# Attention and two MLPs in one kernel: the conversion of the later weights is spread over other steps, and the output products take another order

## The chip, the core and the metric

The kernel runs on one core of a Trainium2 chip. The time is the device time of one execution in microseconds (us), as the median of several runs; a profiled execution gives the trace. The core's engines are TensorE (PE in the rows, its weight loads PEld), VectorE (DVE), ScalarE (ACT), GpSimd (POOL) and SyncE (SP), which issues all DMAs of this kernel. Each engine works through its instructions in the order in which the program wrote them.

## The reference

Three stages, all in float32, with weights that are stored as 64-bit floats:

```
k_p, v_p = mean of k, v over groups of 8 positions        # 576 -> 72 keys
attn = softmax(q k_p^T / 8) v_p                           # 8 batches x 8 heads x 576 positions x 64
x = attn as 4608 tokens x 512
x = (sigmoid(x w_gate) * (x w_val)) w_out                 # 512 -> 1536 -> 512
h = x w2_in                                               # 512 -> 2048
out = (h * cos(h)) w2_out                                 # 2048 -> 512
```

## The kernel before

**Tiling.** The 4608 tokens are worked in nine chunks of 512, numbered 0 to 8 (`c`). To keep float32 precision on TensorE each operand is split into a high and a low part of a shorter type, and each product is three matmuls: high by high, high by low, low by high. Making the parts is a cast on ScalarE (the high part) and a subtraction on VectorE (the low part, `split_lo`, L66). A 64-bit weight first goes through one more ScalarE instruction (`stage_exponent`, L143) and two bit operations on VectorE (`stage_bits`, L148 and L153).

**Gate stage (span 0 to 917).** For each chunk twelve gate steps run (`gv_step`), one for each block of 128 of the 1536 columns: 24 matmuls, a sigmoid on ScalarE, a product on VectorE. Gate and value sums have four PSUM banks together, two steps' worth. Beside the steps of chunk `c` the attention of chunk `c+1` is computed; what stands beside which step is written down by `plan`. At the end of a chunk the attention output goes through a last product (`px`), a cast and a subtraction into `xT`, from which the next chunk's gate products are made. Results go to DRAM (`gd`, `od`), those of chunks 1 to 8 in the sums that a Strassen-Winograd product needs (seven half-size products instead of eight), which GpSimd makes (`tg`).

**Far weights.** While chunks 1 to 7 run, the weights of the later stages are converted: the two output weights (`o2`, 16 blocks, and `o`, 12 blocks) and the cosine weight `i2` (16 blocks), two blocks at a time. For the output weights four Winograd sums of the pair are made on GpSimd and split as well. Everything is stored to DRAM (`wd`, `so`, `td`) and read back later. The generator `far_weights` is cut into half steps by `yield`; `far_step` first issues the stores that are ready and then runs one half step, once ahead of each gate step and once behind it, 24 times a chunk. A pair of `o2` or `o` takes eight half steps, a pair of `i2` six: 14 x 8 + 8 x 6 = 160 of the 168 there are. It works in four slots, `w24` to `w27` (each 4 KB a partition): raw blocks `a` in `w24` and `b` in `w25`, the four sums in `w26`, the split blocks one after the other in `w27`, and then the split sums in `w24` and `w25`, so that the next pair's loads into these wait for the stores of the sums.

**Chunk 8 of the gate stage** has no attention beside it. As its gate and value blocks are used for the last time, `refill` loads far weights into their slots: 12 blocks of `o`, then 16 of `i2`, the first four into `w24` to `w27` ahead of the chunk. Beside it the `o` products of chunk 0 run (`o_step`), from parts that the class `Ahead` fetches and splits.

**Cosine stage (917 to 1607).** For each chunk 16 steps (`h_step`): twelve matmuls (L838 to L840), a reduction of the angle, sine, square and a product. Beside chunks 0 to 6 the `o` products of the later chunks run in 84 units (`unit_go` fetches, casts to `up` and subtracts; `unit_step` multiplies). Beside chunks 7 and 8 the output products of chunk 0 run, one `y_step` behind every second step from step 3 of chunk 7 on (L1046 to L1048, parts `hp`), and three behind the last cosine step. At its last `y_step` four results `y` are copied out of PSUM into the four buffers `r` and stored.

**Output stage (from 1609).** `y_chunk` works chunks 1 to 8 with seven Winograd products each (L1026, L1031), in the order of `PRODUCTS`: accumulators A, B, A, C, A, B, A. `strip` prepares the operand `sp` two products ahead (a cast, L928, and a subtraction). Sums that are needed later are copied to `m` (`kept`, L959) in buffers `r` or `n`; results go to `y` in two buffers `sums`, which the cosine stage used for its own Winograd sums `s`.

Of the kernel before, what the change touches and what calls it, by code (L numbers as in the profile page):

```python
# [23 lines left out]
def attention_two_mlps(  # L24
# [22 lines left out]
    nc = tc.nc  # L47
# [16 lines left out]
    def split_lo(engine, lo, x, hi):  # L64
# [21 lines left out]
    sd = {c: dp.tile([7, P, PAIRS, HALF], F32, name=f"sd{c}") for c in range(1, NC)}  # L86
    wd = {
        (kind, j): dp.tile([P, 2, DM], F32, name=f"w{kind}_{j}")
        for kind, n in (("o2", NF2), ("o", NF), ("i2", NF2)) for j in range(n)
    }  # L90
    td = [dp.tile([P, 4, 2, HALF], F32, name=f"td{m}") for m in range(PAIRS)]

# [84 lines left out]

    def far_weights():

        def tile_(k, shape, dtype, name):  # L180
            return wp.tile(shape, dtype, tag=f"w{2 * NF + k}", name=name)

        def finished(k, kind, j, raw):
            t = tile_(k, [P, 2, DM], F32R, f"w{kind}_{j}")
            nc.scalar.copy(t[:, 0], words(raw, F32, 1))
            yield
            split_lo(nc.vector, t[:, 1], words(raw, F32, 1), t[:, 0])
            t = t.bitcast(F32)
            ready.append((wd[kind, j], t))
            if kind != "o":  # L190
                return
            if j < HF:
                ready.append((so[0][:, j], t[:, :, :HALF]))
            else:
                ready.append((so[5][:, j - HF], t[:, :, :HALF]))
                ready.append((so[6][:, j - HF], t[:, :, HALF:]))

        todo = [("o2", m, PAIRS) for m in range(PAIRS)] + [("o", m, HF) for m in range(HF)]
        todo += [("i2", m, PAIRS) for m in range(PAIRS)]
        for kind, m, step in todo:  # L200
            ja, jb = m, m + step
            a = load((wp, f"w{2 * NF}"), (kind, ja))
            yield
            b = load((wp, f"w{2 * NF + 1}"), (kind, jb))
            stage_exponent(a)
            yield
            stage_exponent(b)
            yield
            stage_bits([a, b])
            yield  # L210
            if kind == "i2":
                yield from finished(3, kind, ja, a)
                both = finished(2, kind, jb, b)
                next(both)
                yield
                next(both, None)
                continue
# [4 lines left out]
            sums = (  # L222
                ((ALU.subtract, a2, a1), (ALU.subtract, b2, t[:, 0]),
                 (ALU.subtract, b2, a2), (ALU.subtract, b1, t[:, 1])) if kind == "o2" else
                ((ALU.add, a2, b2), (ALU.subtract, t[:, 0], a1),
                 (ALU.subtract, a1, a2), (ALU.subtract, b1, t[:, 1]))
            )
            for k, (op, x, y) in enumerate(sums):
                nc.gpsimd.tensor_tensor(out=t[:, k], in0=x, in1=y, op=op)
            yield from finished(3, kind, ja, a)  # L230
            yield
            both = finished(3, kind, jb, b)
            next(both)
            for k in range(2):
                c = tile_(k, [P, 2, 2, HALF], F32R, f"t{kind}{m}_{k}")
                nc.scalar.copy(c[:, :, 0], t[:, 2 * k:2 * k + 2])
                yield
                if k == 0:
                    next(both, None)
                split_lo(nc.vector, c[:, :, 1], t[:, 2 * k:2 * k + 2], c[:, :, 0])  # L240
                c = c.bitcast(F32)
                if kind == "o2":
                    ready.append((td[m][:, 2 * k:2 * k + 2], c))
                else:
                    ready.extend((so[1 + 2 * k + i][:, m], c[:, i]) for i in range(2))

    def split(upto=None, n=2):

# [11 lines left out]
        stage_bits(some)  # L260
        done["bits"] += len(some)

    refills = [("o", f) for f in range(NF)] + [("i2", j) for j in PAIRED]

    def refill(tag):
        kind, j = refills.pop(0)
# [618 lines left out]
    def load_combined(m):  # L885
# [80 lines left out]
    def y_chunk(c, work):  # L966
# [13 lines left out]

        def after(n):

            if n in (0, 1, 2):
                which, name = (("A", "m1"), ("B", "m5"), ("A", "m6"))[n]
                for u in range(2):
                    keep[name, u] = kept(acc[which][u], f"{name}_{c}_{u}")
                if n == 0:
                    y[:] = [
                        hp_.tile([P, 2, C], F32, tag="sums", name=f"y{c}_{r}", bufs=2)
                        for r in range(2)  # L990
                    ]
                return
            if n < 6:
                which, name, rows, cols = {
                    3: ("C", "m1", 0, 0), 4: ("A", "m5", 1, 1), 5: ("B", "m6", 0, 1),
                }[n]
# [41 lines left out]
    def y_step(c, j, g):  # L1038
        w = block("o2", j)
        wh, wl = w[:, 0], w[:, 1]  # L1040
        if j == 0:
            po[c] = [bank("t", [P, DM], f"py{c}_{n}") for n in range(4)]
        for n in range(4):
            p = po[c][n]
            s = slice(n * P, (n + 1) * P)
            nc.tensor.matmul(p, g[:, 0, s], wh, start=j == 0, stop=False)  # L1046
            nc.tensor.matmul(p, g[:, 0, s], wl, start=False, stop=False)
            nc.tensor.matmul(p, g[:, 1, s], wh, start=False, stop=j == NF2 - 1)  # L1048
            if j == NF2 - 1:
                y = hp_.tile([P, DM], F32, tag="r", name=f"y{c}_{n}", bufs=4)  # L1050
                if n % 2:
                    nc.scalar.mul(y, p, -1.0)
                else:
                    nc.vector.tensor_scalar(
                        out=y, in0=p, scalar1=-1.0, scalar2=None, op0=ALU.mult
                    )
                nc.sync.dma_start(out[c * C + n * P:c * C + (n + 1) * P, :], y)

    with tc.manual_schedule():
# [89 lines left out]
        for c in range(NC):  # L1149
            last = c == NC - 1  # L1150
            beside = [[] for _ in range(NF)]
            if not last:
                steps, early = plans[c]
                for n in range(NF):
                    if c == 0:
                        beside[n] += early[n]
                    beside[n] += steps[n]
                    if c + 1 < NC - 1:
                        beside[n] += plans[c + 1][1][n]
            else:  # L1160
# [4 lines left out]
                for n in range(2 * NF, NSLOT):  # L1165
                    refill(f"w{n}")
                at.release()
                mp = tc.alloc_tile_pool(name="mp", bufs=1, side="left", reuse_waits="tile")
                pp[0] = tc.alloc_tile_pool(name="pp1", bufs=1, side="left", reuse_waits="tile")
            for at_f, f in enumerate(FOLDED if c else range(NF)):  # L1170
                tick()
# [5 lines left out]
                elif last:  # L1177
                    if at_f == NF - 1:
# [2 lines left out]
                            name="pp2", bufs=1, side="left", reuse_waits="tile"  # L1181
                        )
                    (unit_go if at_f == NF - 1 else go.go)()
                else:
                    split()
                    far_step()
                gv_step(c, f, 1 if c == 0 and f < FIRST else None)
                if last:
                    for kind in "gv":
                        refill(place[kind, f][1])  # L1190
                    for n in range((0, 0, 0, 1, 1, 1, 2, 2, 2, 2, 1, 0)[at_f]):
                        if n:
                            go.go()
# [30 lines left out]
        for c in range(NC):  # L1224
# [8 lines left out]
            for k, j in enumerate(PAIRED):  # L1233
# [2 lines left out]
                    unit_go()  # L1236
                else:
                    gy.go()
                if c and len(spare) < len(last_slots) and (c >= NC - 2 or k % 4 == 3):
                    load_last()  # L1240
                late.append(h_step(c, j))
                if len(late) > 1:
# [64 lines left out]
```

## Time and profile before

| | us |
|---|---|
| median of 3 runs (1940.66 to 1946.33) | 1942.33 |
| the profiled execution's own time | 1939.25 |
| its span, first to last instruction | 1937.4 |
| TensorE busy | 1794.7 (93%) |
| VectorE busy | 1128.1 (58%) |
| ScalarE busy | 908.8 (47%) |
| GpSimd busy | 548.7 (28%) |
| DMA: 414.28 MB, share of 16 engines | 66.0% |

The page gives busy time, so a stage in which an engine is 100% busy and one in which it waits are mixed in one share. The mean granted clock of TensorE is 0.962 of full speed (2.4 GHz); its other level is 1.2 GHz. The sixteen blocks of `i2` are stored and read back as `wi`, 32 transfers of 512 KB.

### The profile page before, as it was taken

The numbers are of one execution on the slowest core, as the hardware profiler recorded it, in microseconds if no ns is written. First come the engines' busy times: TensorE is split into PE (matmuls) and PEld (weight loads), VectorE is DVE, ScalarE is ACT, GpSimd is POOL, SyncE is SP. The second block draws the span as 40 slices with busy tenths as digits, with TensorE's granted clock in tenths as the row PEclk, the third lists the DMA queues.
The fourth block names the chain that finished last, engine by engine and source line by source line (L and its number), as shares of the span: only waits on it lengthen the run. The fifth ranks groups of instructions, "written<-read, shape, count | busy, mean of one in ns | idle before, by whom it ended". The sixth has DMA issues, their size and how long they took to land. (4 is left out here: it accounts for less than half of the span.)

```text
span 1937.4 us, 24756 instructions
## 1 busy us (share of the span) xinstructions
PE 1794.7 (93%) x8560; PEld 1496.4 (77%) x8560; DVE 1128.1 (58%) x1830; ACT 908.8 (47%) x1528; POOL 548.7 (28%) x656
## 2 busy tenths in 40 slices
PE   5888989888887999999889999999999998999999
PEld 4767867766775778888677888888887886888887
DVE  7675555555545575512456586686685654665565
ACT  6554435343434454411445556556554554444443
POOL 4104352625344332121001334334333441000000
PEclk8989989998988999999999999999999998999999
DMA  8435465647655665586776877877776678666664
GB/s 220 144 118 170 155 213 170 207 155 222 204 190 194 214 198 166 181 290 203 241 239 226 289 255 249 260 257 252 255 235 202 209 253 281 222 220 208 214 221 153
DMA packets 296350, 414.28 MB, mean 214 GB/s; under 512 B 55072, under 2 KB 231712, under 8 KB 296224
## 3 DMA queue, kind: packets, MB, share of 16 engines
q1 hardware_dynamic: 296224, 412.69, 66.0%
q8 instruction: 68, 1.11, 0.2%
q14 instruction: 58, 0.48, 0.1%
HBM read 250.61 MB, written 162.00 MB: 213 GB/s over the span
## 5 line engine op out<-in xcount | busy, mean ns | idle before, releaser
L553 DVE TENSOR_TENSOR g<-pv,g 128x512 f32<-128x512 f32 (+1 forms) x111 | 75.1, 676 | 336.8 <-ACT g L552 141.4
L844 DVE SCALAR_TENSOR_TENSOR r<-n,ph 128x512 f32<-128x512 int32 x144 | 98.9, 687 | 224.5 <-issue 98.1
L838 PE MATMUL ph<-x,wi 128*128 128x512 f32 x576 | 224.1, 389 | 0.0
L839 PE MATMUL ph<-x,wi 128*128 128x512 f32 x576 | 224.1, 389 | 0.0
L840 PE MATMUL ph<-x,wi 128*128 128x512 f32 x576 | 224.1, 389 | 0.0
L545 PE MATMUL pg<-xT,wg 128*128 128x512 f32 (+1 forms) x444 | 188.4, 424 | 35.2 <-ACT xT L529 30.8
L872 POOL TENSOR_TENSOR s<-r,r 128x256 f32<-128x256 f32 x64 | 76.1, 1188 | 453.6 <-DVE r L854 328.3
L850 ACT ACTIVATE r<-r 128x512 f32<-128x512 f32 x144 | 91.1, 633 | 237.2 <-DVE r L847 97.5
L66 DVE TENSOR_TENSOR sp<-sf,sp 128x1024 fp32r<-128x1024 f32 x112 | 133.0, 1229 | 94.8 <-ACT sp L928 94.8
L547 PE MATMUL pg<-xT,wg 128*128 128x512 f32 (+1 forms) x444 | 178.3, 402 | 1.2 <-DVE wg L66 1.2
L546 PE MATMUL pg<-xT,wg 128*128 128x512 f32 (+1 forms) x444 | 179.3, 404 | 0.0
L545 PE MATMUL pv<-xT,wv 128*128 128x512 f32 (+1 forms) x444 | 170.6, 384 | 0.0
L547 PE MATMUL pv<-xT,wv 128*128 128x512 f32 (+1 forms) x444 | 170.5, 384 | 0.0
L546 PE MATMUL pv<-xT,wv 128*128 128x512 f32 (+1 forms) x444 | 170.4, 384 | 0.0
L928 ACT CAST sp<-sf 128x1024 fp32r<-128x1024 f32 x112 | 112.3, 1055 | 75.3 <-PE py_A L1031 28.6
L545 PEld LDWEIGHTS pg<-xT,wg 128*128 128x128 f32 x444 | 89.3, 201 | 54.2 <-ACT xT L529 31.9
L1026 PE MATMUL py_A<-tc,sp 128*128 128x512 f32 x384 | 122.5, 401 | 5.9 <-ACT sp L928 5.9
L838 PEld LDWEIGHTS ph<-x,wi 128*128 128x128 f32 x576 | 108.2, 188 | 22.5
L840 PEld LDWEIGHTS ph<-x,wi 128*128 128x128 f32 x576 | 108.1, 188 | 22.5
L839 PEld LDWEIGHTS ph<-x,wi 128*128 128x128 f32 x576 | 108.1, 188 | 22.4
L552 ACT ACTIVATE g<-pg 128x512 f32<-128x512 f32 (+1 forms) x111 | 64.9, 585 | 116.6 <-PE pg L547 61.2
L847 DVE SCALAR_TENSOR_TENSOR r<-n,r 128x512 f32<-128x512 int32 x144 | 107.8, 749 | 5.0
(180 smaller groups left out, 4160.8 us busy)
## 6 DMA issues: line engine op xcount, KB each, us to landing
sf<-sd SPq DMA_DIRECT2D x112, 512.0 KB
so<-so SPq DMA_DIRECT2D x84, 512.0 KB
uf<-od SPq DMA_DIRECT2D x168, 256.0 KB
sd<-s SPq DMA_DIRECT2D x64, 512.0 KB
wo<-wo SPq DMA_DIRECT2D x56, 512.0 KB
od<-tg SPq DMA_DIRECT2D x48, 512.0 KB
wi<-wi SPq DMA_DIRECT2D x32, 512.0 KB
sd<-r SPq DMA_DIRECT2D x64, 256.0 KB
```

The source lines that it names most:

```text
L66: engine.tensor_tensor(out=lo, in0=x, in1=hi.bitcast(F32), op=ALU.subtract)
L545: nc.tensor.matmul(p, wh, x[:, 0, kb], start=kb == 0, stop=False)
L546: nc.tensor.matmul(p, wh, x[:, 1, kb], start=False, stop=False)
L547: nc.tensor.matmul(p, wl, x[:, 0, kb], start=False, stop=kb == KB - 1)
L838: nc.tensor.matmul(p, wh, x[kb][:, 0], start=kb == 0, stop=False)
L839: nc.tensor.matmul(p, wh, x[kb][:, 1], start=False, stop=False)
L840: nc.tensor.matmul(p, wl, x[kb][:, 0], start=False, stop=kb == KB - 1)
L844: nc.vector.scalar_tensor_tensor(out=r, in0=n, scalar=-C1, in1=p, op0=ALU.mult, op1=ALU.add)
L847: nc.vector.scalar_tensor_tensor(out=r, in0=n, scalar=-C2, in1=r, op0=ALU.mult, op1=ALU.add)
L850: nc.scalar.activation(r, r, AF.Sin, scale=0.5)
L928: nc.scalar.copy(t[:, 0, h * w:(h + 1) * w], got[c, n, h])
L1026: nc.tensor.matmul(p, x[:, 0, m, s], w, start=fresh and m == 0, stop=False, skip_group_check=True,)
```

## The change

The far conversion takes only the two output weights and gives each pair twelve half steps. Both raw blocks load in the first; nothing is done in the second. The four sums are written by GpSimd into the words of the raw blocks that the bit operations have used up (every second word). Split blocks and split sums take turns in `w26` and `w27`, with an empty half step behind the blocks and two behind the sums:

```diff
-        todo += [("i2", m, PAIRS) for m in range(PAIRS)]
         for kind, m, step in todo:
             ja, jb = m, m + step
-            a = load((wp, f"w{2 * NF}"), (kind, ja))
+            a, b = (load((wp, f"w{2 * NF + i}"), (kind, j)) for i, j in enumerate((ja, jb)))
             yield
-            b = load((wp, f"w{2 * NF + 1}"), (kind, jb))
+            yield
             stage_exponent(a)
-            yield
             stage_exponent(b)
             yield
             stage_bits([a, b])
             yield
...
-            t = tile_(2, [P, 4, HALF], F32, f"t{kind}{m}")
+            t = [words(x, F32, 0)[:, h * HALF:(h + 1) * HALF] for x in (a, b) for h in range(2)]
...
             for k, (op, x, y) in enumerate(sums):
-                nc.gpsimd.tensor_tensor(out=t[:, k], in0=x, in1=y, op=op)
-            yield from finished(3, kind, ja, a)
+                nc.gpsimd.tensor_tensor(out=t[k], in0=x, in1=y, op=op)
+            first = plain(2, kind, ja, a)
             yield
-            both = finished(3, kind, jb, b)
...
+            plain_low(kind, ja, first)
+            second = plain(3, kind, jb, b)
+            yield
+            plain_low(kind, jb, second)
+            yield
+            yield
+            first = summed(2, 0, kind, m, a)
+            yield
+            summed_low(0, kind, m, first)
+            second = summed(3, 1, kind, m, b)
+            yield
+            summed_low(1, kind, m, second)
+            yield
+            yield
```

`plain` and `summed` make the cast into slot 2 (`w26`) or 3 (`w27`), `plain_low` and `summed_low` the subtraction, and queue the stores.

The cosine weights are no longer stored and read back. `i2_weights` loads them in chunk 8 into four places of a buffer that the first stage's output tiles use later (`x2`), converts them and writes them straight to the slots where `h_step` reads them: `w24` to `w27`, then the slots that the last six gate steps give free (`refill` hands these over once the twelve `o` blocks are placed). It is called twice a gate step, and once a cosine step of chunk 0:

```diff
+        for n, j in enumerate(PAIRED):
+            at = n if n < 4 else 11 + 5 * (n - 4) // 4
+            for later, fn, args in (
+                (4, low, (n, j)), (0, begin, (n, j)), (2, convert, (n,)), (3, high, (n, j)),
+            ):
+                events.setdefault(at + later, []).append((fn, args))
+        order_ = {low: 0, high: 1, convert: 2, begin: 3}
+        for n in range(max(events) + 1):
+            for fn, args in sorted(events.get(n, ()), key=lambda e: order_[e[0]]):
+                fn(*args)
+            yield
...
                     (unit_go if at_f == NF - 1 else go.go)()
+                    next(i2)
...
                     for kind in "gv":
                         refill(place[kind, f][1])
+                    next(i2)
...
+                if c == 0:
+                    next(i2, None)
+                elif len(spare) < len(last_slots) and (c >= NC - 2 or k % 4 == 3):
                     load_last()
```

`begin` is the load, `convert` the exponent and the two bit operations, `high` the cast and `low` the subtraction. The first four blocks begin at calls 0 to 3, the other twelve at calls 11 to 24.

In the output stage the second and the fourth product change places, C before B; chunk 0's `y` goes into the two buffers `sums`, two results in each; and its first output product stands behind step 5 of cosine chunk 7, so that four stand behind the last cosine step:

```diff
-        ("A", 0, "b11"), ("B", 1, 0), ("A", 2, 1), ("C", 5, "b21"),
+        ("A", 0, "b11"), ("C", 5, "b21"), ("A", 2, 1), ("B", 1, 0),
...
-                y = hp_.tile([P, DM], F32, tag="r", name=f"y{c}_{n}", bufs=4)
+                if n % 2 == 0:
+                    pair = hp_.tile([P, 2, DM], F32, tag="sums", name=f"y{c}_{n}", bufs=2)
+                y = pair[:, n % 2]
...
-                elif k % 2 and (k > 1 if not last else k < 13):
+                elif k % 2 and (k > 3 if not last else k < 13):
```

## Rows read from the trace of the kernel before

**Rows 1.** Busy us (instructions) of each engine by stretch, TensorE's clock, DMA

```profile
146.00:647.00 501.00, 433.31 (x2023) 357.79 (x2022) 268.69 (x536) 208.55 (x368) 219.02 (x263) 0.91 0.60 190
647.00:739.00 92.00, 86.25 (x414) 70.35 (x414) 57.69 (x112) 43.35 (x76) 33.25 (x42) 0.96 0.59 184
739.00:819.00 80.00, 80.00 (x397) 67.39 (x395) 44.75 (x92) 36.25 (x61) 18.85 (x24) 1.00 0.56 181
819.00:917.00 98.00, 98.00 (x434) 81.16 (x433) 18.98 (x28) 16.51 (x29) 18.42 (x24) 1.00 0.77 252
```

**Rows 2.** TensorE's waits, us, times, longest: 146 to 739, then chunk 6 alone

```profile
PE pg L545 <- ACT xT L529: 30.8, 5, 7.8
PE psc L419 <- ACT qT L408: 16.2, 3, 7.3
...
PE pg L545 <- ACT xT L529: 3.1, 1, 3.1
```

**Rows 3.** ScalarE's waits for DMAs over the whole span, us, times, longest

```profile
ACT raw_o L143 <- DMA raw_o<-in_moe_w_out_dram: 108.1, 24, 9.3
ACT raw_i L143 <- DMA raw_i<-in_moe_w_in_dram: 42.2, 13, 6.0
ACT wo L185 <- DMA so<-wo: 29.8, 6, 8.1
```

**Rows 4.** Timeline in chunk 5: start, us, instruction, [idle before <- released by]

```profile
556.89 0.84 SPq L176 DMA_DIRECT2D so<-to  x2
561.89 0.33 SPq L128 DMA_DIRECT2D raw_o<-in_moe_w_out_dram  x1
565.54 0.67 ACT L143 ACTIVATE raw_o<-raw_o 128x512 f32<-128x512 f32 x1 [3.77 <-DMA raw_o<-in_moe_w_out_dram]
...
598.61 1.81 PE L419 MATMUL psc<-kbd,qT 128*128 128x144 f32 x6 [7.33 <-ACT qT L408]
```

**Rows 5.** Instructions on the raw `o` blocks: ns min/median/max, first and last start

```profile
L143 ACT ACTIVATE raw_o<-raw_o x28: 652/667/690, 155.1 to 602.9; 128x512 f32<-128x512 f32 x28
L153 DVE SCALAR_TENSOR_TENSOR raw_o<-raw_o x28: 679/685/1225, 164.6 to 605.9; 128x512 int32<-128x512 int32 x28
L229 POOL TENSOR_TENSOR to<-raw_o x14: 852/1180/1318, 165.3 to 608.4; 128x256 f32<-128x256 f32 x14
```

**Rows 6.** Busy times as in rows 1, at the start of chunk 8

```profile
822.00:835.00 13.00, 13.00 (x59) 10.78 (x58) 3.40 (x6) 3.06 (x5) 2.88 (x4) 1.00 0.90 288
```

**Rows 7.** TensorE's timeline at the start of the cosine stage

```profile
936.34 0.79 PE L794 MATMUL po_A<-up,so 128*128 128x512 f32 x1 [3.39 <-ACT up L754]
...
948.95 0.50 PE L795 MATMUL po_B<-up,so 128*128 128x512 f32 x1 [0.93 <-DVE up L66]
```

**Rows 8.** Timelines of VectorE and TensorE at the first output products

```profile
1487.54 1.89 DVE L66 TENSOR_TENSOR hp<-h,hp 128x512 fp32r<-128x512 f32 x3
1488.27 0.80 PE L1048 MATMUL py<-wo,hp 128*128 128x512 f32 x1 [4.12 <-DVE hp L66]
...
1491.42 0.39 PE L1046 MATMUL py<-wo,hp 128*128 128x512 f32 x1
1491.65 0.40 PE L1047 MATMUL py<-wo,hp 128*128 128x512 f32 x1
```

**Rows 9.** Busy times as in rows 1, behind two waits of TensorE

```profile
1488.00:1491.50 3.50, 3.23 (x8) 2.59 (x9) 3.31 (x6) 1.52 (x4) 0.07 (x1) 0.52 0.97 339
1629.00:1634.80 5.80, 5.62 (x16) 4.32 (x17) 4.72 (x4) 3.90 (x6) 0.00 (x0) 0.50 0.50 138
```

**Rows 10.** The chain that ended last (first row), timelines of TensorE and ScalarE at the handover

```profile
1615.32 4.80 DMA sd<-s
...
1622.31 0.73 PE L1026 MATMUL py_B<-tc,sp 128*128 128x512 f32 x2 [2.64 <-DMA tc<-td]
...
1626.92 1.23 ACT L959 COPY m<-py_A 128x512 f32<-128x512 f32 x2 [7.34 <-DMA out_dram<-y]
...
1629.14 1.22 PE L1026 MATMUL py_A<-tc,sp 128*128 128x512 f32 x2 [5.87 <-ACT sp L928]
...
1634.81 0.63 PE L1026 MATMUL py_A<-tc,sp 128*128 128x512 f32 x2
```

More of the change, by code (lines that the diff above doesn't have):

```diff
@@ L88, in attention_two_mlps @@
         (kind, j): dp.tile([P, 2, DM], F32, name=f"w{kind}_{j}")
-        for kind, n in (("o2", NF2), ("o", NF), ("i2", NF2)) for j in range(n)
+        for kind, n in (("o2", NF2), ("o", NF)) for j in range(n)
     }
@@ L178, in far_weights, with place_, high @@
     def far_weights():
-        def tile_(k, shape, dtype, name):
+        def place_(k, shape, dtype, name):
             return wp.tile(shape, dtype, tag=f"w{2 * NF + k}", name=name)
-        def finished(k, kind, j, raw):
-            t = tile_(k, [P, 2, DM], F32R, f"w{kind}_{j}")
-            nc.scalar.copy(t[:, 0], words(raw, F32, 1))
-            yield
-            split_lo(nc.vector, t[:, 1], words(raw, F32, 1), t[:, 0])
-            t = t.bitcast(F32)
+        def high(k, shape, name, x, hi):
+            t = place_(k, shape, F32R, name)
+            hi = hi(t)
+            nc.scalar.copy(hi, x)
+            return t, x, hi
@@ L189, in finished, with low, plain, plain_low @@
+        def low(t, x, hi, lo):
+            split_lo(nc.vector, lo(t), x, hi)
+            return t.bitcast(F32)
+        def plain(k, kind, j, raw):
+            return high(k, [P, 2, DM], f"w{kind}_{j}", words(raw, F32, 1), lambda t: t[:, 0])
+        def plain_low(kind, j, made):
+            t = low(*made, lambda t: t[:, 1])
             ready.append((wd[kind, j], t))
-            if kind != "o":
-                return
-            if j < HF:
+            if kind == "o" and j < HF:
                 ready.append((so[0][:, j], t[:, :, :HALF]))
-            else:
+            elif kind == "o":
@@ L195, in finished, with summed, summed_low @@
                 ready.append((so[5][:, j - HF], t[:, :, :HALF]))
                 ready.append((so[6][:, j - HF], t[:, :, HALF:]))
+        def summed(k, n, kind, m, raw):
+            return high(
+                k, [P, 2, 2, HALF], f"t{kind}{m}_{n}",
+                words(raw, F32, 0).rearrange("p (o n) -> p o n", o=2), lambda t: t[:, :, 0],
+            )
+        def summed_low(n, kind, m, made):
+            t = low(*made, lambda t: t[:, :, 1])
+            if kind == "o2":
+                ready.append((td[m][:, 2 * n:2 * n + 2], t))
+            else:
+                ready.extend((so[1 + 2 * n + i][:, m], t[:, i]) for i in range(2))
@@ new lines, in far_weights, with i2_weights, begin, convert @@
+            second = plain(3, kind, jb, b)
[11 more added lines that the diff above has]
+            yield
+    free_i2 = []
+    def i2_weights(hold):
+        made = {}
+        def begin(n, j):
+            raw = hold[:, n % 4]
+            nc.sync.dma_start(
+                raw.rearrange("p (kb c) -> p kb c", kb=KB),
+                w2_in[:, j * P:(j + 1) * P].rearrange("(kb p) c -> p kb c", p=P),
+            )
+        def convert(n):
+            stage_exponent(hold[:, n % 4])
+            stage_bits([hold[:, n % 4]])
+        def high(n, j):
+            tag = free_i2.pop(0)
+            t = wp.tile([P, 2, DM], F32R, tag=tag, name=f"wi2{j}")
+            nc.scalar.copy(t[:, 0], words(hold[:, n % 4], F32, 1))
+            made[j] = t
+            place["i2", j] = wp, tag
+        def low(n, j):
+            t = made.pop(j)
+            split_lo(nc.vector, t[:, 1], words(hold[:, n % 4], F32, 1), t[:, 0])
+            blocks["i2", j] = t
+        events = {}
+        for n, j in enumerate(PAIRED):
[9 more added lines that the diff above has]
+            yield
@@ L261, in split @@
         done["bits"] += len(some)
-    refills = [("o", f) for f in range(NF)] + [("i2", j) for j in PAIRED]
+    refills = [("o", f) for f in range(NF)]
     def refill(tag):
+        if not refills:
+            free_i2.append(tag)
+            return
         kind, j = refills.pop(0)
@@ L981, in after @@
         def after(n):
[L983 to L984 removed]
+            if n in (0, 2, 3):
+                which, name = {0: ("A", "m1"), 2: ("A", "m6"), 3: ("B", "m5")}[n]
                 for u in range(2):
@@ L1164, in attention_two_mlps @@
                 far_stores()
-                for n in range(2 * NF, NSLOT):
-                    refill(f"w{n}")
+                free_i2.extend(f"w{n}" for n in range(2 * NF, NSLOT))
                 at.release()
                 mp = tc.alloc_tile_pool(name="mp", bufs=1, side="left", reuse_waits="tile")
+                i2 = i2_weights(
+                    mp.tile([P, 4, 512], I64, tag="x2", name="raw_i2", bufs=2)
+                )
                 pp[0] = tc.alloc_tile_pool(name="pp1", bufs=1, side="left", reuse_waits="tile")
```

32 lines of the change are left out of this document (5 added, 27 removed).

## The prediction

> **What bounds the kernel now.** I read the page first, then the busy times by stretch, then what TensorE waited for, then the timelines of the stretches that have waits. TensorE is the engine that decides: in chunk 7 (739 to 819) it is busy 80.00 of 80.00 us, in chunk 8 98.00 of 98.00, at a granted clock of 1.00 [rows 1]. Where it isn't full, something is to be had. Chunks 1 to 5 (146 to 647) take 501 us with 433.31 busy, so 67.7 idle, and the clock there is 0.91; chunk 6 takes 92 us with 5.75 idle and a clock of 0.96 [rows 1]. All six do nearly the same products. What differs is the far conversion beside them: the pairs of the two output weights in chunks 1 to 5, the cosine weights alone in chunk 6. From 146 to 739 the largest waits of TensorE are for ScalarE: 30.8 us for `xT` and 16.2 for `qT`; in chunk 6 alone 3.1 for `xT` [rows 2].
>
> ScalarE has little work there (208.55 busy of 501), but it works in program order, and it stands still for DMAs of the far conversion: 108.1 us for raw loads of the output weight, 29.8 for stores out of w27, which has to be empty before the next block is written into it [rows 3]. One pair shows the chain: the stores of the converted sums leave at 556.89, the load into the slot that one of them empties only at 561.89 (SyncE stood still between), ScalarE's exponent instruction waits for it until 565.54. In the next pair ScalarE again waits for a load, `qT` comes behind it, and TensorE idles 7.33 us, until 598.61 [rows 4].
>
> **Part 1, the far pairs.** Instructions per pair stay: 2 exponents, 4 casts, 4 bit operations, 4 subtractions, 4 GpSimd sums. Three waits go. The next loads go into w24 and w25, which now hold the sums in place and are last read by a subtraction two half steps earlier, so no load stands behind a store. Both loads start a whole gate step before the first exponent (some 8 us; 92 us by 12 steps [rows 1]); the one that left at 561.89 had landed by 565.54, 3.7 us [rows 4]. Each cast into w26 or w27 comes two half steps after the store that empties it, again a gate step. At the end of a chunk the last half step only stores, so that nothing of the far work stands on ScalarE ahead of the `xT` casts. The sums are written with a gap of one word; the trace has no such GpSimd write. I cost it between 0 and as much as the sum itself again, 1.2 us each (L229, up to 1.18 [rows 5]); with four sums a pair and two gate steps before the cast that reads them, I take 0.
>
> Fourteen pairs by 12 half steps are 168, just the 7 chunks by 24, so chunks 1 to 7 all carry two pairs each, where before 1 to 5 carried three and 6 four cosine pairs. That is less than chunk 6 carried on ScalarE and VectorE, and chunk 6 still waited on raw cosine loads (42.2 us in all over 13 waits [rows 3]). Chunk 6 is therefore my model: 92 us at most. Its floor is chunk 6 without its loss of clock: 4% of 92 us is 3.7, so 88.3 with all its waits (80, as in chunk 7, is out of reach, since that has no keys and values and one tile less [rows 1]). I take 91.5 for five of them and 89.5 for chunk 3, which has one tile less: 547 against 593, that is -46. If nothing but chunk 6's own rate comes, 6 by 92.5 (the page's stretches are cut to whole us), it is -38; if the floor comes, -593 + 6 x 88.3 = -63. Chunk 7 carries heavier pairs than before beside a TensorE without idle time: +0.5 (0 to +2).
>
> **Part 2, the cosine weights.** Sixteen stores and sixteen reloads of 512 KB go, 16.8 MB of 414; DMA isn't the limit of the gate chunks (share 0.60 [rows 1]), so this is worth nothing there by itself. In chunk 8 and the first cosine steps ScalarE gets 16 exponents and 16 casts (0.667 for both, 21 us), and VectorE 32 bit operations and 16 subtractions (0.685 for all, 33 us) [rows 5]. Twelve or thirteen sixteenths fall into chunk 8, where VectorE is busy 18.98 and ScalarE 16.51 of 98 us [rows 1]: hidden, as long as no instruction blocks. The block that can is the exponent, which waits for a raw load and stands ahead of the sigmoid. At the chunk's start four raw loads (2.1 MB) come on top of what goes there now, while the four reloads ahead of the chunk go and later ones move. The stretch 822 to 835 moved 288 GB/s at a DMA share of 0.90 [rows 6], 3.7 MB; 5.8 would take 20 us, so that the fourth load lands some 7 us late and a sigmoid about 4 us. One gate step here is 24 matmuls at 0.23 [rows 8], 5.5 us, and the gate and value products of two steps fit into their four banks, so that TensorE has a gate step of slack: +1 (0 to +6).
>
> The Trainium skill (DMA: Bandwidth & Descriptors, Specifications) puts what a core can move to and from HBM at about 358 GB/s; a short stretch with 339 at a share of 0.97 [rows 9] comes near that, the 288 at 0.90 don't. By its figure the same 5.8 MB would take 16 us, the last load would be 3 us late and the term 0, so the sum 1 us less; I go by the rows.
>
> In the first five cosine steps the rest comes on two engines on which TensorE already waits: 3.39 us for the cast `up`, then 0.93 for its subtraction in every second unit [rows 7]. A step gets 1.3 us more of ScalarE and 1.9 of VectorE, four times. Nothing hidden would be 4 x 1.9 = +8, all hidden 0: I take +4. On the other side SyncE is no longer held by reloads that wait for the last gate products, which could pull the 3.39 in; I leave it as the lower bound, -3.
>
> **Part 3, the output products start two steps later.** In chunk 7 of the cosine stage TensorE waits 4.12 us for the first `hp`, and the next seven matmuls, from 1488.27 to 1491.42, stand 0.45 apart where those behind stand 0.23; the granted clock is 0.52 in that stretch, nearly all of it the lower level (1.2 GHz) [rows 9]. 1.5 us more, together 5.6. The three `hp` subtractions start at 1487.54 [rows 8]. Two cosine steps of 2.7 us (twelve matmuls at 0.23) put ahead bring TensorE there at about 1489, when two of the three are done. -5 (-3 to -6). The product left out comes in the tail, the same work.
>
> **Part 4, the handover to the output products.** TensorE waits 2.64 us for the last `tc` load and 5.87 for `sp`, and the 5.67 us from 1629.14 to 1634.81 carry four blocks of which one takes 0.7 at full clock (two matmuls of 512 and two of 256 columns, 0.23 and 0.12), at a clock of 0.50 [rows 9]: 2.9 more, 11.4 us in all. The cast `sp` stands behind `m`, which is written to a buffer that `y` has left to its store, and waits for that store until 1626.92 [rows 10]. Now `y` takes the two `sums` buffers, and `m1` finds its own free. The second pair of `y` has to wait for the last `sd<-s` store, which left at 1615.32 and landed 4.8 us later; with four products in the tail this comes one product, 2.7 us, earlier against TensorE: 1617.5 in the old clock. Then come the copy of `y`, two of `m` and one cast: some 1620.5, and TensorE ends the second product at 1620.2. C as second product needs no `tc`, so that the 2.64 go. Late next is the subtraction behind that cast, 1.2 us. 11.4 less about 2.4 is -9 (-11 to 0, when the wait only changes its buffer). In the steady part the order of products changes nothing that TensorE waits for: 0.
>
> **Sum.** -46 + 0.5 + 1 + 4 - 5 - 9 = -54.5. The profiled execution took 1939.25 us with a span of 1937.4, which gives 1885; its time is 3 us under the median of the runs, so 1888.
>
> **Rivals.** First, the wait at the chunk's end stays. The 30.8 us for `xT` are the largest share of TensorE's waits [rows 2], and the chain of product, cast, subtraction and next product is there without any far work; chunk 6 shows it at 3.1, with cosine casts on ScalarE. If it stays at 7, four to five boundaries keep 4 us and the low clock after it (1.5 as in rows 8), some 25 us: gate chunks at -21 and 1913. Against it: ScalarE's own rows put a far cast directly ahead of `xT`.
>
> Second, the handover's wait only moves: `y` now waits for the `sums` store, and the first output tile for the four `y` stores, which took until 1626.9. Without Part 4's gain the time is 1897. For it speaks that two DMAs stand in a row there, against it that the first is three steps old.
>
> Third, the slower end: the cosine weights stall ScalarE. All 16 exponents in chunk 8 wait for loads in a stretch that starts at 288 GB/s [rows 6], and each holds back a sigmoid or a cosine cast. The longest wait on a raw cosine load was 6.0 us, the mean 3.2 [rows 3]. With one gate step of slack already spent, 16 by 4 us is 64 in place of the 5 above, and the time 1947; it decides from 3.7 us a block on (54.5 and 5, by 16). Against it: after the fourth block no load is begun for seven half steps, and ScalarE has 80 us to spare.
>
> A fourth, that the new pauses change nothing because another wait of the gate chunks was as late (keys on GpSimd, scores on VectorE), would leave only the tail's -14, and the upper bounds of the cosine weights (6 + 8 + 2) take these back: 1944. Chunk 6 speaks against it.
>
> **How the numbers follow.** Forecast 0.60, with 1873 to 1905 as its own bounds; first rival 0.19; second 0.10; third 0.07; fourth 0.04. Under 0.3% (6 us) this kernel can't be told from unchanged. The first three are faster (0.89), the third rival slower (0.07), the fourth within 0.3% (0.04). The range reaches from near the floor of the gate chunks (1871; with the lower bound of the cosine start 1864), 1868, to the first rival with the upper bounds of the cosine start, 1922.
>
> **What would show it.** Right: no wait of ScalarE for `so<-wo` or `wo<-wo`, raw waits under 30 us in all, chunks 1 to 6 near 91 us with TensorE at a clock of 0.96 or more; no wait of 4 us at the first `hp`; `m` without a wait for `out_dram<-y`. Wrong: `xT` waits of 7 us still there; idle time of TensorE in chunk 8; over 10 us of it in the first five cosine steps.

## The result and the profile after

The changed kernel takes 1829.3 us (median of 4 runs, 1827.95 to 1830.81) against 1941.51 for the kernel before on the same chip (median of 4): 0.942 of before, 95% interval 0.940 to 0.944. The change is about twice the 54.5 us that were forecast, and it lies below the range. The span fell by 109.2 us, from 1937.4 to 1828.2. Split at the start of the last sigmoid of each gate chunk, then of the first cast `n` of a cosine chunk and of the first product of the output stage (us):

| stretch | before | after | difference | forecast |
|---|---|---|---|---|
| to the end of chunk 0 | 145.8 | 147.8 | +1.9 | 0 |
| gate chunks 1 to 6 | 593.5 | 490.3 | -103.2 | -46 |
| chunk 7 | 79.4 | 79.4 | 0 | +0.5 |
| chunk 8 | 97.9 | 97.9 | 0 | +1 |
| cosine chunk 0 | 125.7 | 127.3 | +1.5 | +4 |
| cosine chunks 1 to 6 | 434.8 | 434.9 | 0 | 0 |
| cosine chunks 7 and 8 with the last of chunk 0's products | 131.8 | 133.1 | +1.4 | -5 |
| output stage | 328.3 | 317.5 | -10.8 | -9 |

Chunk 0 does the same as before; over the profiles of the changed kernel and its variants below its end lies between 146.0 and 148.8, so its +1.9 is taken as scatter. What is left is one large term, the gate chunks, and the handover. The busy times of the same stretches as in [rows 1], of the changed kernel (us of the stretch, then busy us and instructions of TensorE, its weight loads, VectorE, ScalarE, GpSimd, then the granted clock, DMA share, GB/s):

```profile
148.00:556.00 408.00, 405.36 (x2025) 339.67 (x2024) 251.37 (x499) 196.17 (x340) 199.44 (x248) 1.00 0.60 189
556.00:638.00 82.00, 82.00 (x413) 67.84 (x412) 50.14 (x102) 40.95 (x72) 36.72 (x47) 1.00 0.62 200
638.00:717.00 79.00, 79.00 (x391) 66.57 (x391) 47.35 (x91) 36.48 (x60) 26.18 (x34) 1.00 0.52 178
717.00:815.00 98.00, 98.00 (x434) 81.17 (x433) 41.21 (x63) 30.40 (x52) 20.63 (x24) 1.00 0.80 268
```

Chunks 1 to 5 hold the same products as before (2025 records for 2023) in 408 us in place of 501, and TensorE is busy 405.36 of them at a clock of 1.00, where it had 433.31 of 501 at 0.91. Busy time itself went down by 28 us: before, part of it was matmuls at the lower clock. Chunk 8 has VectorE at 41 us for 19 and ScalarE at 30 for 17 [rows 1], and TensorE is as full as it was. What TensorE waited for from 148 to 717, all of it, against [rows 2]:

```profile
PE px L584 <- DVE aT L66: 2.6, 1, 2.6
```

ScalarE's waits for DMAs there, against [rows 3] (us, times, longest):

```profile
ACT raw_o L143 <- DMA raw_o<-in_moe_w_out_dram: 16.0, 13, 3.7
ACT to L186 <- DMA wo<-wo: 12.2, 6, 3.1
ACT to L186 <- DMA so<-wo: 3.4, 3, 2.1
```

They didn't vanish, but they make only 31.6 us (with 4.5 more for `raw_i`, from chunk 8 on), each is short, and none reaches TensorE. Before, the far conversion's waits were longer than [rows 3] shows, since its rows leave out the other stores from `w27`:

```profile
ACT wo L185 <- DMA wo<-wo: 29.4, 6, 8.5
```

With them it was 209.5 us over the whole span, 20.2 of the 42.2 for `raw_i` in chunk 6 and 14.9 in chunk 7.

### The profile page after: what moved, and what is told of

Same layout as the page of the kernel before. It is cut to its first block, busy times and chain, and to the rows that moved or that the text cites. A ratio compares the mean times of both kernels' runs of the same rounds, so it can differ in the third digit from the quotient of the medians.

```text
span 1828.2 us, 24685 instructions
## 1 busy us (share of the span) xinstructions
PE 1764.3 (97%) x8560; PEld 1477.5 (81%) x8560; DVE 1135.8 (62%) x1830; ACT 913.0 (50%) x1528; POOL 542.5 (30%) x656
## 5 line engine op out<-in xcount | busy, mean ns | idle before, releaser
L66 DVE TENSOR_TENSOR sp<-sf,sp 128x1024 fp32r<-128x1024 f32 x112 | 132.9, 1229 | 80.8 <-ACT sp L984 80.7
L601 PE MATMUL pg<-xT,wg 128*128 128x512 f32 (+1 forms) x444 | 179.8, 405 | 2.0 <-ACT e L519 2.0
L603 PE MATMUL pg<-xT,wg 128*128 128x512 f32 (+1 forms) x444 | 172.7, 389 | 1.1 <-DVE wg L66 1.1
L602 PE MATMUL pg<-xT,wg 128*128 128x512 f32 (+1 forms) x444 | 172.3, 388 | 0.0
L66 DVE TENSOR_TENSOR up<-uf,up 128x1024 fp32r<-128x1024 f32 x84 | 102.4, 1219 | 6.2 <-ACT up L810 6.2
```

The lines of the kernel that those rows point to most:

```text
L66: engine.tensor_tensor(out=lo, in0=x, in1=hi.bitcast(F32), op=ALU.subtract)
L601: nc.tensor.matmul(p, wh, x[:, 0, kb], start=kb == 0, stop=False)
L602: nc.tensor.matmul(p, wh, x[:, 1, kb], start=False, stop=False)
L603: nc.tensor.matmul(p, wl, x[:, 0, kb], start=False, stop=kb == KB - 1)
```

## Experiments

All are the changed kernel with one edit, unless said. Times are medians of two to five runs; the kernel before ran beside each on the same chip, at 1943 to 1947.

**e1: the old pair code, cosine weights still in chunk 8**

`far_weights` is that of the kernel before, without the cosine weights. Against that kernel:

```diff
-        todo += [("i2", m, PAIRS) for m in range(PAIRS)]
...
-            if kind == "i2":
...
-                continue
```

> The changed kernel, but with the pair code of before for the two output weights (eight half steps, old slots); the cosine weights stay in chunk 8. Theory A: each old pair stops ScalarE on its own loads and stores, and that costs TensorE idle time and then its clock. Then chunks 1 to 4 stay at 97 to 101 us as before, chunk 5 at some 95 (its last third is free), chunks 6 and 7, now without any far work, come to 80 to 82 and 79; the time is some 1915 us. Rival B: the cosine conversion with its stores and reloads was what loaded the gate stage; then chunks 1 to 5 fall to 90 or less and the time is under 1880. Chunk 6 also tells whether its 92.5 us of before were its own products and waits (it stays above 88) or the cosine conversion (80 to 83).

1928.04 us, 0.991 of before (95% interval 0.987 to 0.994). The chunks 1 to 7 take 101.4, 97.9, 103.5, 101.0, 100.1, 82.8 and 79.4 us.

```profile
147.00:651.00 504.00, 436.24 (x2023) 360.14 (x2022) 266.06 (x531) 206.65 (x363) 217.35 (x264) 0.91 0.59 187
651.00:734.00 83.00, 83.00 (x418) 68.69 (x417) 38.63 (x89) 34.40 (x60) 28.73 (x41) 1.00 0.34 102
```

Theory A holds, though the time is 13 us over its 1915: chunk 3 is slower than it said, and chunk 5, whose last third is free, takes 100.1 for some 95. Moving the cosine weights gives chunks 1 to 5 nothing. It gives chunk 6 everything: without far work it takes 83 us and TensorE doesn't idle, so its 92 us [rows 1] were no floor but the cosine conversion of before. That is the number on which the forecast stood.

**e2 and e5: the old slots, spaced**

The old pair code with empty half steps; the edit is shown against that code (e1):

```diff
             b = load((wp, f"w{2 * NF + 1}"), (kind, jb))
-            stage_exponent(a)
             yield
+            yield
+            stage_exponent(a)
             stage_exponent(b)
...
             yield from finished(3, kind, ja, a)
             yield
+            yield
...
+            yield        # e2: three, e5: two
+            yield
```

> As the changed kernel with the old slots (sums in w26, split blocks both in w27, split sums in w24 and w25), but with twelve half steps: one more behind the loads, one behind the first store, three at the end. Theory A1: spacing alone is enough, since every cast and load then comes a gate step or more behind the DMA that it needs; chunks 1 to 6 at 80 to 84 us, time 1828 to 1842. Rival A2: the slots matter, since loads still go where stores have to leave first; chunks at 86 to 92, time 1865 or more.

1854.25 us: chunks 1 to 6 at 80.8 to 83.9, but chunk 8 at 113.0. The edit had made thirteen half steps a pair.

> The kernel of e2 with two empty half steps at the end of a pair in place of three. That one took thirteen half steps a pair (182 of the 168 there are), so that the last pair was converted at once at the start of chunk 8, which took 113 us for 98. Theory: with twelve, chunk 8 comes back to 98 and chunks 1 to 6 stay at 80 to 84 us, time 1832 to 1842; spacing alone then brings nearly all of the gate stage's gain. Rival: what chunks 1 to 6 gained in e2 came from the thirteenth half step, and they rise to 86 or more, time over 1855.

1828.68 us: chunks 1 to 6 at 490.2 us together, chunk 8 at 97.9. Spacing alone does all that the change does to the gate stage; the new slots and the sums in place aren't needed for it.

**e3: the new slots without the empty half steps**

```diff
             yield
-            yield
             stage_exponent(a)
...
             plain_low(kind, jb, second)
             yield
-            yield
...
             summed_low(1, kind, m, second)
-            yield
-            yield
```

> The changed kernel without its four empty half steps, so eight half steps a pair in the new slots, chunks 1 to 5 carrying three pairs. Theory A1 (spacing decides): the exponent stands half a gate step, about 3.5 us, behind a load that takes 5 to 8 us to land, and the casts one half step behind the stores; chunks 1 to 4 at 93 to 101 us, time 1890 to 1915. Rival A2 (the slots decide): loads no longer stand behind stores, so that chunks 1 to 4 come to 82 to 88, time 1835 to 1860.

1874.44 us; chunks 1 to 5 at 87.6, 93.5, 86.9, 90.8 and 93.2. Neither number was met: with pairs as dense as before, the new pair code (slots, sums in place, both loads first) is worth half. What TensorE waited for in chunks 1 to 5:

```profile
PE pg L597 <- ACT xT L581: 19.1, 4, 6.5
PE px L580 <- ACT qT L460: 5.6, 2, 4.3
PE psc L471 <- ACT qT L460: 3.4, 3, 1.6
PE px L580 <- DVE aT L66: 3.4, 2, 2.1
PE px L580 <- ACT aT L560: 0.9, 1, 0.9
```

e3 and e1 also tell waits from work. In chunks 1 to 5 both run the same number of instructions (VectorE 531, ScalarE 364 and 363), e3 as follows:

```profile
147.00:599.00 452.00, 419.57 (x2023) 348.22 (x2022) 260.85 (x531) 209.48 (x364) 210.52 (x263) 0.96 0.65 208
```

ScalarE's waits for the far conversion's DMAs there, e1 and then e3:

```profile
ACT raw_o L143 <- DMA raw_o<-in_moe_w_out_dram: 95.9, 22, 9.5
ACT wo L185 <- DMA so<-wo: 31.6, 6, 8.1
ACT wo L185 <- DMA wo<-wo: 29.4, 6, 8.6
...
ACT raw_o L143 <- DMA raw_o<-in_moe_w_out_dram: 47.2, 19, 6.0
ACT to L186 <- DMA so<-wo: 31.9, 7, 7.7
ACT to L186 <- DMA wo<-wo: 21.2, 8, 6.0
```

They fall from 156.9 us to 100.3, and TensorE's idle time from 67.8 to 32.4, with as much work beside it.

**e6 and e7: one empty half step moved to the end of the pair**

```diff
             yield
-            yield                    # e6: behind the loads
             stage_exponent(a)
...
             plain_low(kind, jb, second)
             yield
-            yield                    # e7: behind the first stores
...
+            yield                    # both: at the end
```

> The changed kernel with the empty half step behind the loads moved to the end of the pair, so that the two exponents come one half step, 3 to 4 us, behind loads that land in 5.0 to 8.5 us (median 6.4). ScalarE's waits for raw loads rise from 16 us to 60 to 100. Theory A: such a wait stands ahead of a sigmoid and costs TensorE what goes over its gate step of slack, little in itself; chunks 1 to 6 rise by 0 to 4 us each, time 1830 to 1853. Rival: pauses don't matter behind loads (the gain is the stores'), time within 2 us of the changed kernel, 1829.

> The changed kernel with the empty half step behind the first stores moved to the end of the pair, so that the cast of the sums into w26 comes one half step, 3 to 4 us, behind the issue of the store that empties it. ScalarE's waits for wo<-wo and so<-wo rise from 14 us to 40 to 70. Theory A: chunks 1 to 6 rise by 1 to 4 us each, time 1833 to 1853, more than e6, since the wait can hold a cast of the attention too. Rival: within 2 us of 1829.

1824.20 and 1829.86 us; chunks 1 to 6 at 487.4 and 488.0. Both theories A fall: ScalarE waits longer for stores in e7 (33.6 us from 148 to 632 in place of 13.4), and TensorE doesn't notice. In e6 the raw waits rose only to 24.1 us, not to 60. Its time is below the rival's too (1827 to 1831), but 3.9 of the 6.6 us by which its span is shorter lie in chunk 0 and cosine chunk 0, which the edit doesn't touch.

**e11 and e12: all empty half steps at the end**

```diff
-            yield                    # e12 only: the four of the change
...
+            for _ in range(4):       # at the end of the pair;
+                yield                # e11: code of e1, e12: new slots
```

> The old pair code and the old slots, its eight half steps as dense as before, then four empty ones; cosine weights in chunk 8. Theory D (the number of pairs in a chunk decides): two pairs a chunk stop ScalarE as long each as before (some 12 us), but TensorE has time to catch up in the empty steps and none of it falls on the xT casts at the chunk's end; chunks 1 to 6 at 82 to 88 us, time 1830 to 1865. Theory S (the distance inside a pair decides): a wait of 4 to 9 us costs TensorE the same wherever it stands, two thirds of the 100 us of loss remain; chunks at 92 to 96, time 1890 to 1910.

> The new slots with all four empty half steps at the end of the pair, the eight others as dense as in e3. Theory D: chunks 1 to 6 at 80 to 83 us, time within 5 us of the changed kernel, 1824 to 1834. Theory S: the waits of e3 stay (100 us of ScalarE's in 14 pairs), chunks at 84 to 87, time 1850 to 1862.

1835.36 and 1825.41 us. Theory D holds: what counts is how far apart the pairs are, hardly where the pause stands inside one. In e11 the code of a pair is that of before, word for word, and TensorE idles 3.7 us in chunks 1 to 5 instead of 67.7.

```profile
148.00:558.00 410.00, 406.29 (x2028) 339.78 (x2027) 250.94 (x499) 195.41 (x340) 200.22 (x246) 1.00 0.59 188
```

ScalarE's waits for DMAs in the same stretch of e11:

```profile
ACT raw_o L143 <- DMA raw_o<-in_moe_w_out_dram: 21.9, 9, 5.6
ACT wo L185 <- DMA wo<-wo: 21.6, 5, 6.7
ACT wo L185 <- DMA so<-wo: 7.3, 2, 5.0
```

Single waits of 5 to 6.7 us are still there, and pass. What changed is that the raw waits fell from 108.1 us for 14 pairs [rows 3] to 21.9 for some ten. By the code a pair's loads no longer stand right behind the last stores of the pair ahead.

**e13: ten half steps**

```diff
-            for _ in range(4):       # of e12
+            for _ in range(2):
                 yield
```

> New slots, eight half steps and two empty ones at the end, so 140 of 168 half steps and a pair that no longer ends with a chunk. Theory T (a threshold: what stays inside TensorE's gate step of slack is free): chunks 1 to 5 at 80 to 83 us as with twelve, chunk 6 partly and chunk 7 wholly without far work, time 1822 to 1832. Theory L (the loss falls in proportion to the pairs in a chunk): chunks 1 to 5 half way between e3 (90 on the mean) and twelve (81), at 84 to 87, time 1842 to 1855. If waits of TensorE for xT appear at some chunk ends only, the place of the pair against the chunk's end is a part of it.

1855.54 us; chunks 1 to 5 at 84.1, 84.4, 85.7, 95.9 and 82.5, 86.5 on the mean: as theory L has it. But the loss isn't spread evenly. Chunks 1 to 5, and what TensorE waited for there:

```profile
149.00:581.00 432.00, 412.01 (x2020) 342.59 (x2020) 245.76 (x514) 202.20 (x351) 203.33 (x254) 0.98 0.61 195
...
PE pg L599 <- ACT xT L583: 11.7, 3, 6.9
PE psc L473 <- ACT qT L462: 4.3, 1, 4.3
PE px L582 <- DVE aT L66: 2.0, 2, 1.7
PE px L582 <- ACT qT L462: 1.1, 1, 1.1
PE px L582 <- ACT aT L562: 0.8, 1, 0.8
```

Ten half steps move a pair's place from chunk to chunk. ScalarE's timeline shows the end of chunk 2, where TensorE then waits 6.86 us for `xT`, and that of chunk 4, where it doesn't wait:

```profile
323.61 0.65 ACT L186 CAST to<-raw_o 128x512 fp32r<-128x512 f32 x1 [5.73 <-DMA wo<-wo]
324.17 1.40 ACT L583 CAST xT<-px 128x320 fp32r<-128x320 f32 x4
...
502.04 1.66 ACT L583 CAST xT<-px 128x192 fp32r<-128x192 f32 x4 [2.51 <-PE px L582]
```

A far cast that waits for a store stands ahead of all four casts of `xT` in the first; in the second `xT` waits for its own products alone. At the end of chunk 3 it is a raw load (6.1 us of wait, TensorE 4.35). So place and number count together, and a test that separates them wasn't made.

**e4, e8, e9, e10: the output products**

```diff
-                elif k % 2 and (k > 3 if not last else k < 13):      # e4
+                elif k % 2 and (k > 1 if not last else k < 13):
...
-        ("A", 0, "b11"), ("C", 5, "b21"), ("A", 2, 1), ("B", 1, 0),  # e8
+        ("A", 0, "b11"), ("B", 1, 0), ("A", 2, 1), ("C", 5, "b21"),
...
-                if n % 2 == 0:                                       # e9
-                    pair = hp_.tile([P, 2, DM], F32, tag="sums", name=f"y{c}_{n}", bufs=2)
-                y = pair[:, n % 2]
+                y = hp_.tile([P, DM], F32, tag="r", name=f"y{c}_{n}", bufs=4)
...
-                else:                                                # e10
+                elif c > NC - 2 or k != 1:
                     gy.go()
```

e8 also puts the copies behind the products back into their old places.

> The changed kernel with the first output product back behind step 3 of cosine chunk 7. The prediction gave this move 5 us, so the time would be 1834. Theory: the move only changed which matmul waits, since ScalarE stands still for the four fetches of hd either way; TensorE then waits about 4 us at the first product in place of 4.04 us in front of a cosine product, and the time is that of the changed kernel within 2 us (1828 to 1831).

1830.92 us, within the scatter of the changed kernel. TensorE waits 4.2 us at the first `hp` again and no longer 4.0 at a cosine product, and the handover has 3.8 us of waits for 0.7; by the stretches the later start is worth 2.6 us (output stage 317.5 for 321.1, the stretch ahead of it 133.1 for 132.1), where the fourth product in the tail shortens the handover's waits.

> The changed kernel with the old order of the output products (B second, C fourth), y still in the two sums buffers. Theory: the second product again needs the last tc load, 2.6 us of wait, and m5 is copied ahead of the strips, so the handover costs 3 to 5 us more and nothing else changes: 1832 to 1835. Rival: the order does nothing, since four products in the tail already cover the tc load: 1829 within 1 us.

1826.21 us: the order of the products does nothing that can be measured. TensorE doesn't wait for `tc` in the old order either; that the fourth product in the tail covers the load is likely, but no run tests it.

> The changed kernel with the last results y of chunk 0 back in the four buffers r, everything else changed. Theory: the copy to m1 again waits for a y store to land (7.3 us before), the strip behind it on ScalarE too, and the handover costs 7 to 10 us more: 1834 to 1839. Rival: with a fourth product in the tail and C in second place the stores are early enough, within 2 us of 1829.

1835.78 us, with the output stage at 324.5 us for 317.5. The copy to `m` waits for a `y` store again, and TensorE for the strip behind it:

```profile
ACT m L1015 <- DMA out_dram<-y: 7.2, 1, 7.2
...
1526.72 1.22 PE L1082 MATMUL py_A<-tc,sp 128*128 128x512 f32 x2 [5.22 <-ACT sp L984]
```

> The changed kernel, leaving out one call of the fetch-and-split of hd in step 1 of cosine chunk 7, so that the casts hp stand two steps behind their loads. Theory: ScalarE's 2 us wait there delayed the reduction chain of the cosine and with it TensorE (4.04 us and the low clock after it, some 1.5); both go, cosine chunk 7 is 4 to 6 us shorter and the time 1823 to 1825. Rival: the first output product comes too early for the later casts, the wait moves once more and the time stays within 2 us of 1829.

1825.71 us. By the stretches cosine chunks 7 and 8 are 1.8 us shorter (131.3 for 133.1), where 4 to 6 were expected. In the changed kernel ScalarE waits at the casts `hp` and with it the cosine chain, TensorE behind it; with the casts a step later the wait on the DMA is gone and TensorE's is halved. First two rows: the changed kernel's timeline.

```profile
1382.98 1.28 ACT L710 CAST hp<-h 128x512 fp32r<-128x512 f32 x2 [1.96 <-DMA h<-hd]
1387.76 0.79 PE L894 MATMUL ph<-x,wi 128*128 128x512 f32 x1 [4.04 <-DVE r L910]
```

The same two places in e10:

```profile
1382.09 1.64 ACT L710 CAST hp<-h 128x512 fp32r<-128x512 f32 x3
...
1386.38 0.50 PE L894 MATMUL ph<-x,wi 128*128 128x512 f32 x1 [1.92 <-DVE r L910]
```

**e14 and e15: e12, e8 and e10 together, beside the changed kernel**

> The changed kernel with the four empty half steps at the end of a pair (e12), the old order of the output products (e8) and the later casts hp (e10). If the three add up: e10 takes about 4 us, the other two nothing within noise or up to 3 us; 1819 to 1826, faster than the changed kernel on the same chip.

> The changed kernel itself once more, on the chip of e13 and e14, as their measure: 1826 to 1831.

1820.43 us (0.936, 0.934 to 0.938) beside 1829.63 (0.941, 0.939 to 0.943) on the same chip: 9 us less than the changed kernel, and the fastest of the study. Of the 9.9 us between the two spans 5.4 lie in chunks 1 to 6 and 3.4 in cosine chunks 7 and 8. The first are nearly all chunk 5: 79.4 us in e6, e12 and e14, which have no empty half step behind the loads, for 82.1 to 84.4 in the changed kernel's two profiles and those of e4 and e7 to e10, where TensorE waits there once for `aT`, 2.1 to 2.8 us. In chunks 1 to 5 of e14 it has no wait left:

```profile
146.00:550.00 404.00, 404.00 (x2029) 339.00 (x2028) 243.53 (x499) 197.83 (x340) 189.74 (x246) 1.00 0.60 191
```

The medians of e5 to e8, e12 and e15 lie between 1824 and 1830 on several chips; differences among them are read from stretches only.

## Why the prediction was wrong, point by point

**Direction, place and cause were right.** ScalarE, held in program order by DMAs of the far conversion, delayed `xT` and `qT`, and with them TensorE; that is where 103 of the 109 us went. Between e1 and e3 the amount of work is the same, so what TensorE gained there came with the shorter waits; from three pairs a chunk to two work and waits both fall, and no run separates them there.

**The step that failed is the size of Part 1: "Chunk 6 is therefore my model: 92 us at most", with 88.3 as its floor "with all its waits".** Chunk 6 was measured under the same disease: the cosine conversion, with 20.2 us of waits of its own on ScalarE. e1 shows it at 83 us without, and the changed kernel at 82.5 with two pairs. That its waits (3.1 us for `xT`, 2.7 for `aT`) would stay was never tested against chunk 7, which has both chains and waited for neither [rows 1]. Its rows held the better model: 80.00 us for 397 matmuls, which gives 407.7 us for the 2023 of chunks 1 to 5 and 83.4 for the 414 of chunk 6 (an estimate, since the kinds of matmul differ a little); 408 and 82.5 came. That chunk 7 has less to do, the reason for which it was set aside, is allowed for by the count. The first rival failed for the same reason: in the changed kernel TensorE doesn't wait for `xT` at any chunk's end, and e13 shows it waiting where a far instruction stands ahead.

**The clock was priced from chunk 6 alone.** The forecast took chunk 6's 0.96 as its loss; chunks 1 to 5 stood at 0.91. Set against the 404 us of e14, chunks 1 to 5 lost this much, beside TensorE's idle time in the same stretch:

| kernel | half steps, slots | chunks 1 to 5 | lost | idle | clock |
|---|---|---|---|---|---|
| before | 8, old | 501 | 97 | 67.7 | 0.91 |
| e1 | 8, old | 504 | 100 | 67.8 | 0.91 |
| e3 | 8, new | 452 | 48 | 32.4 | 0.96 |
| e13 | 10, new | 432 | 28 | 20.0 | 0.98 |
| e11 | 12, old | 410 | 6 | 3.7 | 1.00 |
| changed | 12, new | 408 | 4 | 2.6 | 1.00 |

In the first four rows the time lost is 1.4 to 1.5 times the idle time (in the last two the rounding to whole us is too large a part of it). The rest is matmuls at the lower clock, as behind the two waits of [rows 9], where the granted clock was 0.52 and 0.50: TensorE's busy time is 436.24 us in e1 and 404.00 in e14. Idle 67.7 and 5.75 of before [rows 1], 73.4 us, by 1.4 to 1.5 are 103 to 110; 103 came.

**What did it is only in part what the prediction named.** It gave three reasons for the waits to go: new slots, distance inside a pair, and an empty half step at the chunk's end. e5, e11 and e12 show that neither the slots nor the distances inside a pair are needed (e11, which has neither, stands 6 us over the changed kernel, 3 of them in chunks 1 to 7); the step from three pairs a chunk to two, with free half steps between them, is enough. Whether the number of pairs or their place against the chunk's end does more stays open (e13 moves both). Of its signs the raw waits held (16.0 us, under 30), but ScalarE still waits 15.6 us for stores, which was to be nothing.

**Part 2.** Right: most of 16 exponents, 16 casts and 48 VectorE instructions went into chunk 8 and cost nothing there, although the fourth load was thought to hold a sigmoid; the third rival didn't occur. At the start of the cosine stage +1.5 for +4, inside its bounds. The paragraph on the Trainium skill (DMA: Bandwidth & Descriptors, Specifications) had the term at 0 by its limit of about 358 GB/s, and 0 it was, but that limit didn't hold here: the new chunk 8 moved 268 GB/s on the whole and 377 in this stretch of it.

```profile
728.00:748.00 20.00, 20.00 (x90) 16.57 (x89) 10.66 (x18) 7.83 (x14) 3.31 (x4) 1.00 1.04 377
```

(The share adds up the times of packets; over 1, some of them overlap.) The 288 GB/s that the sum went by were no bound either.

**Part 3.** Wrong: -5 became nothing at its place. The three casts `hp` wait for their loads on ScalarE in the kernel before too:

```profile
1482.74 1.29 ACT L654 CAST hp<-h 128x512 fp32r<-128x512 f32 x2 [1.99 <-DMA h<-hd]
```

The cosine chain stands behind them, so that 4.12 us at `hp` [rows 8] became 4.04 at `ph`. The prediction took the start of the `hp` subtractions as given and moved only the product; it didn't ask what held the casts, nor follow the cosine step queued behind them. e10 takes away the DMA wait, and 1.92 of the 4.04 us stay; what holds these wasn't tested.

**Part 4.** Right in size and cause: -10.8 for -9. By the output stage e9 gives 7.0 us of it back by the buffers alone, and e4 3.6 by the fourth product. The second rival's wait is there, at the copy of `y`, but it doesn't hold TensorE, whose waits at the handover are 0.7 us:

```profile
ACT y L1110 <- DMA sd<-s: 5.7, 1, 5.7
```

The order of the products, which was credited with the `tc` wait, has no part in it (e8).

## What to carry to other kernels

A stretch that is to serve as the model of a stretch without a disturbance must be free of its own disturbance: compare the full stretch next to it (chunk 7, TensorE 80 of 80) before its waits are called a floor. Price a wait of TensorE with the clock behind it (here 1.4 to 1.5 us lost for each us of waiting), from busy time at either level and not from idle time alone. On an engine that works in order, first spread work that waits for DMAs over more steps; once there was room, the buffers of the far conversion came to nothing here, and the placing of the pauses to 3 to 5 us in one chunk.

## What the runs showed of the hardware

The 512 KB loads of a raw block landed 5.0 to 8.5 us after their issue in the changed kernel (median 6.4), where the prediction read 3.7 from one of them. GpSimd's sums, which now write every second word and wrote a dense tile before, take no longer in all: the 56 of them took 49.8 us in both kernels, so that the upper bound of 1.2 us a sum, kept for that, wasn't needed. (The 1.18 us behind that bound is the median of its row; the longest sum took 1.32 [rows 5].)
